# The last projection in rows over four column groups, the mean taken off ahead of it, the last gate kept as rows

## The chip, the cores and the metric

The kernel runs on one core of a Trainium2 chip. The metric is the device time of one execution in microseconds (us). TensorE is called PE here (its weight loads PEld), VectorE DVE, ScalarE ACT, GpSimd POOL and SyncE SP. SP issues all DMA transfers of this kernel. SBUF tiles have 128 partitions; matrix products go to PSUM, which has eight banks of 512 f32 per partition.

## The reference

One decode step of a block with two halves, for a batch of four tokens (B = 4, D = 512). `c` gives six modulation vectors; the first half is attention with 32 heads over a cache of 4096 keys, the second a gated MLP with F = 1792 (half of it, Fh, is 896).

```python
mod = (_silu(c) @ w_mod).reshape(c.shape[0], 6, 1, -1)
sa, ca, ga, sb, cb, gb = (mod[:, 0].copy(), ..., mod[:, 5].copy())
h = _layernorm(x, axis=-1) * (1 + ca) + sa
x = x + ga * _A_ref(h, A_k_cache, A_v_cache, A_wq, A_wo)
h = _layernorm(x, axis=-1) * (1 + cb) + sb
x = x + gb * _B_ref(h, B_w_in, B_w_sp, B_b_sp, B_w_out)

def _B_ref(x, w_in, w_sp, b_sp, w_out):          # one token: S = 1
    z = _gelu(jnp.einsum('bsd,df->bsf', x, w_in))
    z1 = z[..., :Fh].copy()
    z2 = _layernorm(z[..., Fh:], axis=-1)
    g = jnp.einsum('ts,bsf->btf', w_sp, z2) + b_sp[None, :, None]
    return jnp.einsum('bsf,fd->bsd', z1 * g, w_out)
```

With one token per batch entry, w_sp and b_sp are single numbers. So the output is x1 + gb * (w_sp * rstd * ((z1 * (z2 - mean)) @ w_out) + b_sp * (z1 @ w_out)), where x1 is x after the attention and mean and rstd are those of z2.

## The kernel before

**Loads.** The caches hold 268 MB and are read in 16 pairs of tiles, one pair for a group of 8 heads of one batch entry, in three large SBUF buffers (`kv[0]` to `kv[2]`) that take turns. Ahead of them come w_mod and wq, which lie in kv[2] first (L335, L417 to L422); behind them come wo, w_in and w_out, in kv[2] again (L663 to L668): wo in three parts, w_in in four (one for each j, 128 rows of the 512), w_out in three (its row tiles 0 to 3, 4 to 5 and 6). kv[0] is free of cache tiles near the end, and the small tiles of the last stages are cut out of it (L346).

**Start.** The six modulation vectors are made by `mod_part` as products of w_mod (stationary, 128 columns at a time) with silu(c) (`sT`), so they come out with the 512 features over the partitions: `modT[:, oc]` is 128 x (4 feature tiles x 4 batch entries). The last of them, the gate gb, is multiplied by w_sp and b_sp into `gwb` (L545). The queries are made next (L546 to L549).

**Attention.** A loop over the tiles (L636): DVE multiplies keys by the query, PE folds them, softmax, PE multiplies values in four column groups (`values`, L605): each product has only 32 stationary columns, and `tile_position=(0, 32 * t)` puts it in one of four strips of the array, with its output in the 32 PSUM partitions below it.

**End.** `output` multiplies by wo; x1 is made with features over the partitions (L715 to L717), with its layer norm. The products with w_in (L742) run over j, then over the two halves (s = 1 is z2, s = 0 is z1), then over seven row tiles jf: 56 products of 128 stationary columns, with 8 moving columns (batch entries twice, for a part with and without rstd), or 4 for the last j. After j = 1 stands one f32 product (L753) that transposes x1 into rows, 16 x 128, one row for a batch entry and feature tile; DVE copies them to `xr` (L757). GELU on ACT gives z2 (L761) and z1 (L763). DVE spreads z2 over 16 columns (`z2r`, L768), PE sums z2 (L773) and its products with itself (L775), DVE multiplies z1 by z2 into `u[:, :, 0]`, beside z1 in `u[:, :, 1]` (L776), and PE multiplies both with w_out: 28 products with 128 stationary columns of w_out and 8 moving columns (L778). DVE makes mean and rstd (L787 to L801). The result has features over the partitions. One product gives b_sp's part of it, transposed into rows on PE (L812); z1*z2's part less mean times z1's is transposed by another (L823); DVE adds x1 and stores (L822 to L830).

**Order.** Each engine runs its instructions in the order in which the code adds them. `Program.add` (L54) and `depend` (L75) find the waits: `region` (L18) describes each operand by its partitions and the range from its first to its last byte, so a strided view counts with all that lies between its ends, and in PSUM whole banks count for each 32 partitions. PE's instructions signal only where `done` or `sem` says so. `mm` (L384) adds a product with its weight load, `weights` and `moving` the two apart. POOL instructions also wait for the one before last.

Of the kernel before, what the change touches and what calls it, by code (L numbers as in the profile page):

```python
# [7 lines left out]
BF16 = mybir.dt.bfloat16  # L8
# [244 lines left out]
def kernel(  # L253
# [62 lines left out]
    modT = sb.tile([P, 6, J, B], F32, name="modT")  # L316
    qbc = sb.tile([P, NQ, DH], BF16, name="qbc")
    x1b = sb.tile([P, 2, J, B], F32, name="x1b")
# [3 lines left out]
    gwb = sb.tile([P, 3, J, B], F32, name="gwb")  # L322
    sT = sb.tile([P, J, B], BF16, name="sT")


    fill = sb.tile([P, 96], BF16, name="fill")
# [8 lines left out]
    wm, wq, hbc, rows, ones_b, xb, xcT, sg, hn = parts(  # L335
        kv[2], 0, J * 6 * D, J * H * DH, J * B * 64, D, P, *(2 * n * J * B for n in (2, 2, 1, 1)),
    )
    xcT = xcT.bitcast(F32).rearrange("p (j b) -> p j b", j=J)
# [7 lines left out]
    ones_f, ident_f, oP, h, u, zt, z2, z2r, qo, yo, ot, xr, ro, x1p = parts(  # L346
        kv[0], 0, P, 2 * P, 8 * NH // 2 * B, 2 * JB, 2 * JF * B, 4 * JF * B, JF * (B + 4), JF * JB, JB, JB,
        P, 2 * P, 2 * P, 2 * JB,
    )
    ident_f, zt, xr, ro, x1p = (t.bitcast(F32) for t in (ident_f, zt, xr, ro, x1p))  # L350
# [24 lines left out]
    def dve(name, *args, **kw):  # L375
        return prog.call("DVE", name, *args, **kw)
# [82 lines left out]
    for t in (mx, hbc, osb):  # L459
        pool("memset", t, 0.0)  # L460
# [6 lines left out]
        "tensor_reduce", out=maskb[0:J * B], axis=AX.X, op=ADD,  # L467
        in_=ident[0:J * B, 0:J * B].rearrange("p (b j) -> p b j", j=J),
# [233 lines left out]
    pool("memset", z2[:, :, B:B + 1], 1.0)  # L702
# [12 lines left out]
    x1, sq = x1b[:, 0], x1b[:, 1]  # L715
# [14 lines left out]

    rows_ps = {n: bank[0:J * B, 0:P] for n, bank in (("x", po_b), ("c", attn_b), ("a", s_b[2]))}
    rstd = deviation(st, "ln2")
    x1p = x1p.rearrange("p (b j) -> p b j", b=B)
    dve("tensor_copy", out=x1p.rearrange("p b j -> p j b"), in_=x1)
# [51 lines left out]
    zs = sb.tile([P, 8], F32, name="zs")[0:JB]  # L786
    dve(  # L787
        "scalar_tensor_tensor", out=zs[:, 0:B], in0=sq_ps[:, 0:B], scalar=1.0 / FH, in1=maskb[0:JB],
# [4 lines left out]
    total = sb.tile([P, B], F32, name="total")  # L793
    dve("tensor_reduce", out=total, in_=cut(small, JF, B).rearrange("p j b -> p b j"), axis=AX.X, op=ADD)
# [5 lines left out]
    act("activation", out=rstd, in_=zs[:, B + 2:B + 3], func=AF.Ln, bias=eps[0:JB], scale=-1.0)  # L800
    rstd_done = act("activation", out=rstd, in_=rstd, func=AF.Exp, scale=-0.5)  # L801
    dve(
        "scalar_tensor_tensor", out=gwb[:, 1], in0=gwb[:, 0], scalar=-1.0 / FH, in1=bc(total, J),
        op0=MULT, op1=MULT,
    )


    qo, yo = (t.rearrange("p (b j) -> p b j", b=B) for t in (qo, yo))
    dve(
        "tensor_tensor", out=yo.rearrange("p b j -> p j b"), in0=y_ps[:, :, 1], in1=gwb[:, 2], op=MULT,  # L810
    )
    mm(rows_ps["c"], yo.rearrange("p b j -> p (b j)"), ident, True, True, True)  # L812
    dve(
        "tensor_tensor", out=gwb[:, 0:2], in0=y_ps.rearrange("p j e b -> p e j b"), in1=gwb[:, 0:2],
        op=MULT,
    )
    dve(
        "tensor_tensor", out=qo.rearrange("p b j -> p j b"), in0=gwb[:, 0], in1=gwb[:, 1], op=ADD,
    )
    ro, ot = ro[0:JB], ot[0:JB]  # L820

    dve("tensor_tensor", out=ro, in0=rows_ps["c"], in1=xr, op=ADD, after=[rstd_done])  # L822
    mm(rows_ps["a"], qo.rearrange("p b j -> p (b j)"), ident, True, True, True)  # L823
    dve(
        "scalar_tensor_tensor", out=ot, in0=rows_ps["a"], scalar=rstd, in1=ro, op0=MULT, op1=ADD,
    )
    prog.add(
        "SP", lambda e, it: e.dma_start(out=out.rearrange("b s (j p) -> (b s j) p", p=P), in_=ot),
# [49 lines left out]
```

## Time and profile before

| | us |
|---|---|
| median of three runs (662.53 to 662.73) | 662.6 |
| the profiled execution | 662.62 |
| its span in the trace | 660.8 |
| PE / DVE / ACT / POOL busy | 394.6 / 392.7 / 27.3 / 2.6 |
| granted TensorE clock, mean | 0.799 |
| HBM read at 428 GB/s over the span | 282.73 MB |
| last instruction of the program proper (issue of the store) | 658.52 |

Times in the trace count from the start of the span. In the slices of the span, each digit is a busy share, or for PEclk the granted clock, in tenths. A line of the timeline gives start, length, engine, line, operation, output <- inputs and shape; its bracket says how long the engine had been idle and what released it. Nearly all instructions are recorded by helpers, so their line is L160 for DVE and ACT, and L386, L391 and L396 for `mm`, `weights` and `moving`. Tiles cut out of the three large buffers all appear as `kv`, PSUM banks as `bank`. The shape of a product begins with rows * columns of the weights, so `128*32` marks one in a column group. An f32 product appears as two passes.

### The profile page before, as it was taken

The numbers are of one execution on the slowest core, as the hardware profiler recorded it, in microseconds if no ns is written. First come the engines' busy times: TensorE is split into PE (matmuls) and PEld (weight loads), VectorE is DVE, ScalarE is ACT, GpSimd is POOL, SyncE is SP. The second block draws the span as 40 slices with busy tenths as digits, with TensorE's granted clock in tenths as the row PEclk, the third lists the DMA queues.
The fourth block names the chain that finished last, engine by engine and source line by source line (L and its number), as shares of the span: only waits on it lengthen the run. The fifth ranks groups of instructions, "written<-read, shape, count | busy, mean of one in ns | idle before, by whom it ended". The sixth has DMA issues, their size and how long they took to land.

```text
span 660.8 us, 5144 instructions
## 1 busy us (share of the span) xinstructions
PE 394.6 (60%) x2724; PEld 79.7 (12%) x1753; DVE 392.7 (59%) x344; ACT 27.3 (4%) x64; POOL 2.6 (0%) x11
## 2 busy tenths in 40 slices
PE   1628385563848556383855638386563938646875
PEld 1300101010010101001010100101010010101114
DVE  2058292864829386482937648293764829376953
ACT  1100000000000000000000000000000000000002
POOL 1000000000000000000000000000000000000000
PEclk9959787687968768797776879877687987768995
DMA  9999999999999999999999999999999999999996
GB/s 377 446 440 436 414 428 440 436 441 440 428 417 440 436 440 440 428 420 440 436 436 440 436 424 428 440 432 444 432 428 424 440 436 440 436 428 413 438 412 279
DMA packets 7324, 282.86 MB, mean 428 GB/s; under 512 B 780, under 2 KB 916, under 8 KB 2708
## 3 DMA queue, kind: packets, MB, share of 16 engines
q1 hardware_dynamic: 7316, 282.74, 99.1%
q8 instruction: 7, 0.11, 0.1%
q14 instruction: 1, 0.01, 0.0%
HBM read 282.73 MB, written 0.00 MB: 428 GB/s over the span
## 4 chain that ended last, share of the span: by engine, by line
DMA 61%; PE 24%; DVE 12%; another core or an unknown queue 2%; issue 1%; SPq 0%; ACT 0%; DVEq 0%
DMA kv<-in_A_k_cache_dram 57%; PE bank L396 23%; DVE kv L160 12%; DMA kv<-in_A_wo_dram 4%; PE bank L386 1%; SPq L166 0%; DVE S L160 0%; ACT E L160 0%; DVE mx L160 0%; DVE x1b L160 0%; ACT kv L160 0%; DVE rsh L160 0%; DVE mT L160 0%; DVE nm L160 0%
## 5 line engine op out<-in xcount | busy, mean ns | idle before, releaser
L160 DVE TENSOR_TENSOR kv<-kv,qbc 128x8192 bf16<-128x8192 bf16 x64 | 280.2, 4419 | 187.0 <-DMA kv<-in_A_k_cache_dram 187.0
L396 PE MATMUL bank<-kv,ident 128*128 128x512 bf16 x1024 | 259.6, 416 | 162.5 <-DVE kv L160 162.4
L386 PE MATMUL bank<-kv,Ph 128*32 128x512 bf16 x1024 | 89.0, 524 | 0.9 <-DMA kv<-in_A_v_cache_dram 0.9
L160 DVE TENSOR_REDUCE S<-bank 128x64 f32<-128x512 f32 x64 | 43.8, 684 | 36.2 <-PE bank L396 36.2
L386 PE MATMUL bank<-rsh,mean_d 128*128 128x8 f32 x32 | 9.3, 365 | 79.0 <-DVE rsh L160 79.0
L391 PEld LDWEIGHTS <-ident 128*128 128x128 bf16 x65 | 7.7, 118 | 300.9 <-issue 300.9
L160 DVE TENSOR_TENSOR Ph<-E,mask 128x2048 bf16<-128x2048 f32 (+1 forms) x19 | 36.9, 1954 | 10.7 <-ACT E L160 10.7
L386 PEld LDWEIGHTS bank<-kv,Ph 128*32 128x32 bf16 x1024 | 32.9, 127 | 49.6 <-issue 41.0
L160 ACT ACTIVATE E<-S,nm 128x256 f32<-128x256 f32 x16 | 8.1, 507 | 456.7 <-DVE nm L160 456.7
L386 PEld LDWEIGHTS bank<-rsh,mean_d 128*128 128x128 f32 x32 | 7.8, 304 | 141.5 <-DVE rsh L160 141.1
L386 PEld LDWEIGHTS bank<-sel,osb 128*128 128x128 f32 x136 | 17.8, 191 | 55.4 <-issue 54.6
L386 PE MATMUL bank<-sel,osb 128*128 128x8 f32 x136 | 16.3, 246 | 0.4 <-ACT osb L160 0.4
L160 ACT COPY osb<-bank 128x512 f32<-128x512 f32 x16 | 9.4, 586 | 137.5 <-PE bank L386 137.5
L386 PE MATMUL bank<-kv 128*32 128x512 bf16 (+2 forms) x139 | 9.8, 416 | 1.2 <-DMA kv<-in_A_wq_dram 0.8
L396 PE MATMUL bank<-kv,kv 128*128 128x4 bf16 (+1 forms) x212 | 7.0, 168 | 2.4 <-DMA kv<-in_A_wo_dram 2.1
L386 PE MATMUL bank<-ident,kv 8*128 8x8 bf16 (+2 forms) x10 | 0.9, 186 | 11.6 <-DMA kv<-in_A_x_dram 11.3
L391 PEld LDWEIGHTS <-kv 128*128 128x128 bf16 x212 | 6.7, 107 | 3.2 <-DMA kv<-in_A_wo_dram 2.3
L160 DVE TENSOR_REDUCE mx<-S 128x1 f32<-128x256 f32 x16 | 6.7, 420 | 0.5
L160 DVE COPY kv<-bank 128x32 f32<-128x32 f32 (+1 forms) x2 | 0.5, 230 | 9.7 <-ACT kv L160 9.7
L160 DVE RECIPROCAL rz<-bank 128x8 f32<-128x8 f32 x17 | 3.3, 196 | 4.5 <-PE bank L386 4.5
L386 PE MATMUL bank<-sT,kv 128*128 128x4 bf16 x96 | 3.7, 169 | 2.1 <-DVE modT L160 1.8
L386 PEld LDWEIGHTS bank<-kv 128*32 128x32 bf16 (+2 forms) x139 | 4.1, 107 | 6.4 <-issue 2.3
(86 smaller groups left out, 56.2 us busy)
## 6 DMA issues: line engine op xcount, KB each, us to landing
kv<-in_A_k_cache_dram SPq DMA_DIRECT2D x2, 4096.0 KB, 20.2
kv<-in_A_v_cache_dram SPq DMA_DIRECT2D x2, 4096.0 KB, 32.3
kv<-in_A_wq_dram SPq DMA_DIRECT2D x1, 4096.0 KB, 17.9
kv<-in_w_mod_dram SPq DMA_DIRECT2D x1, 3072.0 KB, 10.0
kv<-in_A_wo_dram SPq DMA_DIRECT2D x1, 2560.0 KB, 22.7
kv<-in_B_w_in_dram SPq DMA_DIRECT2D x4, 448.0 KB, 12.9
kv<-in_A_wo_dram SPq DMA_DIRECT2D x1, 1024.0 KB, 24.7
kv<-in_A_wo_dram SPq DMA_DIRECT2D x1, 512.0 KB
```

Source lines behind the costliest of these rows:

```text
L160: return getattr(e, name)(*args, **kw, **(dyn(it) if dyn else {}))
L386: "PE", lambda e, it: e.matmul(out, lhsT=lhsT, rhs=rhs, start=start, stop=stop, **kw),
L391: prog.add("PE", lambda e, it: e.ldweights(lhsT), [lhsT], [], done=False)
L396: return e.add_instruction(mybir.InstMatmult(name=nc.get_next_instruction_name(), engine=mybir.EngineType.PE, ins=[e.lower_ap(rhs), e.lowe ...
```

## The change

The tiles of the last stage get 32 columns for each row tile, of which every eighth holds a batch entry (`cols`) and the others are zero. So a product with 32 stationary columns yields 32 rows, four of them in use, and four such products, one for each quarter t of the 512 output features, fill the four column groups: row 32 t + 8 b holds feature tile t of batch entry b.

- The last gate is made in that form at the start, by 16 products with silu(c) stationary (`sTp`), and copied to `gate` (128 x 128, f32); `modT` holds five vectors and `gwb` is gone.
- x1 goes into rows by four f32 products with `x1p` stationary, at the place of the one before. The copy to `xr` moves behind the products with w_out in the code, and DVE comes to it after the multiply that makes u.
- Sums of z2 are accumulated over jf in four columns (`total`); the sums of squares and of z2 use 28 products in column groups, with no copy of z2.
- DVE takes the mean off z2 (`zc`) before it multiplies by z1.
- Products with w_out have u as the stationary operand and 128 columns of w_out as the moving one, 56 in four column groups: first the part for b_sp (e = 1), then the other (e = 0), for row tiles 0 to 5, then both for row tile 6. They go to two PSUM banks.
- The two banks are multiplied by b_sp or w_sp and the gate, x1 is added, the other part is multiplied by rstd and added, and 16 rows, every eighth, are stored.

```diff
-    modT = sb.tile([P, 6, J, B], F32, name="modT")
+    modT = sb.tile([P, 5, J, B], F32, name="modT")
-    gwb = sb.tile([P, 3, J, B], F32, name="gwb")
-    sT = sb.tile([P, J, B], BF16, name="sT")
+    gate = sb.tile([P, P], F32, name="gate")
...
+    W = 32
+    cols = slice(0, W, W // B)
...
+    sTp = sTp.rearrange("p (j n) -> p j n", j=J)
+    sT = sTp[:, :, cols]
...
-    for t in (mx, hbc, osb):
+    for t in (mx, sTp, hbc, osb):
         pool("memset", t, 0.0)
...
-        "tensor_reduce", out=maskb[0:J * B], axis=AX.X, op=ADD,
-        in_=ident[0:J * B, 0:J * B].rearrange("p (b j) -> p b j", j=J),
+        "tensor_reduce", out=maskb, axis=AX.XY, op=ADD,
+        in_=ident.rearrange("p (t b k) -> p b t k", t=J, b=B),
...
-    for oc in range(2, 6):
+    for oc in range(2, 5):
         mod_part(oc)
+
+    for j in range(J):
+        for t in range(J):
+            c0 = 5 * D + t * P
+            mm(
+                small[W * t:W * t + W, 0:P], sTp[:, j], wm[:, j, c0:c0 + P], j == 0, j == J - 1,
+                j == t == J - 1, tile_position=(0, W * t),
+            )
+    dve("tensor_copy", out=gate, in_=small[:, 0:P])
     mm(cut(small, 2), ones_b, wb_t, True, True, True)
     dve("tensor_copy", out=wbf, in_=cut(small, 2))
-    for k in range(2):
-        dve("tensor_scalar_mul", out=gwb[:, 2 * k], in0=modT[:, 5], scalar1=wbf[:, k:k + 1])
...
-    pool("memset", z2[:, :, B:B + 1], 1.0)
+    u = u.rearrange("p (j e n) -> p j e n", e=2, n=W)
+    x1p = x1p.rearrange("p (j n) -> p j n", j=J)
+    for t in (u, z2, x1p):
+        pool("memset", t, 0.0)
+    pool("memset", z2[:, :, W:W + 1], 1.0)
...
-    dve("tensor_copy", out=x1p.rearrange("p b j -> p j b"), in_=x1)
+    dve("tensor_copy", out=x1p[:, :, cols], in_=x1)
...
             if j == 1 and s == 0:
-                mm(rows_ps["x"], x1p.rearrange("p b j -> p (b j)"), ident_f, True, True, True)
+                for t in range(J):
+                    mm(
+                        po_b[W * t:W * t + W, 0:P], x1p[:, t], ident_f, True, True, t == J - 1,
+                        tile_position=(0, W * t),
+                    )
...
-    xr = xr[0:J * B]
-    dve("tensor_copy", out=xr, in_=rows_ps["x"])
...
-    z2, z2_1 = z2[:, :, 0:B], z2[:, :, 0:B + 1]
-    act("activation", out=z2, in_=zt[:, 1], func=AF.Gelu_apprx_tanh)
-    u = u.rearrange("p (j e b) -> p j e b", e=2, b=B)
-    act("activation", out=u[:, :, 1], in_=zt[:, 0], func=AF.Gelu_apprx_tanh)
+    z1c, z2c = u[:, :, 1, cols], z2[:, :, cols]
+    act("activation", out=z2c, in_=zt[:, 1], func=AF.Gelu_apprx_tanh)
+    act("activation", out=z1c, in_=zt[:, 0], func=AF.Gelu_apprx_tanh)
...
-    z2r = z2r.rearrange("p (j m) -> p j m", j=JF)
+    total = small[:, 0:B]
+    weights(ones_f)
+    for jf in range(JF):
+        moving(total, ones_f, z2c[:, jf], jf == 0, jf == JF - 1, jf == JF - 1)
+    sq_ps = s_b[2][:, 0:B + 1]
+    for jf in range(JF):
+        for t in range(J):
+            mm(
+                sq_ps[W * t:W * t + W], z2[:, jf, 0:W], z2[:, jf, 0:W + 1:W // B], jf == 0, jf == JF - 1,
+                jf == JF - 1 and t == J - 1, tile_position=(0, W * t),
+            )
+    zc = zc.rearrange("p (j b) -> p j b", b=B)
     dve(
-        "tensor_copy", out=z2r.rearrange("p j (b k) -> p j b k", b=B),
-        in_=z2[:, :, :, None].to_broadcast([P, JF, B, J]),
+        "scalar_tensor_tensor", out=zc, in0=bc(total, JF), scalar=-1.0 / FH, in1=z2c, op0=MULT, op1=ADD,
     )
-    sq_ps = s_b[2][0:JB, 0:B + 1]
-    mm(cut(small, JF * B), ones_f, z2, True, True, True)
-    for jf in range(JF):
-        mm(sq_ps, z2r[:, jf], z2_1[:, jf], jf == 0, jf == JF - 1, jf == JF - 1)
-    dve("tensor_tensor", out=u[:, :, 0], in0=u[:, :, 1], in1=z2, op=MULT)
-    y_ps = cut(zo_b, J, 2, B)
-    for j0, j1 in JFS:
-        for jf in range(j0, j1):
-            for jo in range(J):
-                mm2(
-                    y_ps[:, jo], wout[:, jf, jo * P:(jo + 1) * P], u[:, jf],
-                    jf == 0 and jo == 0, jf == JF - 1, jf == JF - 1 and jo == J - 1,
-                )
+    dve("tensor_tensor", out=u[:, :, 0, cols], in0=z1c, in1=zc, op=MULT)
+    y_ps = [zo_b[:, 0:P], attn_b[:, 0:P]]
+    for j0, j1 in ((0, JFS[-1][0]), JFS[-1]):
+        for e in (1, 0):
+            for jf in range(j0, j1):
+                for t in range(J):
+                    mm(
+                        y_ps[e][W * t:W * t + W], u[:, jf, e], wout[:, jf, t * P:(t + 1) * P], jf == 0,
+                        jf == JF - 1, jf == JF - 1 and t == J - 1, tile_position=(0, W * t),
+                    )
+    dve("tensor_copy", out=xr, in_=po_b[:, 0:P])
...
-    total = sb.tile([P, B], F32, name="total")
-    dve("tensor_reduce", out=total, in_=cut(small, JF, B).rearrange("p j b -> p b j"), axis=AX.X, op=ADD)
...
-    dve(
-        "tensor_tensor", out=yo.rearrange("p b j -> p j b"), in0=y_ps[:, :, 1], in1=gwb[:, 2], op=MULT,
-    )
-    mm(rows_ps["c"], yo.rearrange("p b j -> p (b j)"), ident, True, True, True)
...
-    mm(rows_ps["a"], qo.rearrange("p b j -> p (b j)"), ident, True, True, True)
+    for e, t in ((1, t1), (0, t0)):
+        dve(
+            "scalar_tensor_tensor", out=t, in0=y_ps[e], scalar=wbf[:, e:e + 1], in1=gate,
+            op0=MULT, op1=MULT,
+        )
+
+    dve("tensor_tensor", out=t1, in0=t1, in1=xr, op=ADD, after=[rstd_done])
+    dve("scalar_tensor_tensor", out=ot, in0=t0, scalar=rstd, in1=t1, op0=MULT, op1=ADD)
     prog.add(
-        "SP", lambda e, it: e.dma_start(out=out.rearrange("b s (j p) -> (b s j) p", p=P), in_=ot),
+        "SP", lambda e, it: e.dma_start(
+            out=out.rearrange("b s (t n) -> t (b s) n", n=P), in_=ot[::W // B],
+        ),
```

More of the change, by code (lines that the diff above doesn't have):

```diff
@@ L315 @@
     oT = sb.tile([P, 1 + NQ, NH], BF16, name="oT")
-    modT = sb.tile([P, 6, J, B], F32, name="modT")
+    modT = sb.tile([P, 5, J, B], F32, name="modT")
     qbc = sb.tile([P, NQ, DH], BF16, name="qbc")
-    x1b = sb.tile([P, 2, J, B], F32, name="x1b")
     wbm = sb.tile([P, 2 + B], F32, name="wbm")
@@ L321 @@
     xT = sb.tile([P, J, B], F32, name="xT")
-    gwb = sb.tile([P, 3, J, B], F32, name="gwb")
-    sT = sb.tile([P, J, B], BF16, name="sT")
-    fill = sb.tile([P, 96], BF16, name="fill")
+    gate = sb.tile([P, P], F32, name="gate")
+    fill = sb.tile([P, 48], BF16, name="fill")
     kv = [sb.tile([P, NT * DH], BF16, name=f"kv{a}") for a in range(3)]
@@ L332, in parts @@
             a += n
-    wm, wq, hbc, rows, ones_b, xb, xcT, sg, hn = parts(
-        kv[2], 0, J * 6 * D, J * H * DH, J * B * 64, D, P, *(2 * n * J * B for n in (2, 2, 1, 1)),
-    )
+    W = 32
+    cols = slice(0, W, W // B)
+    wm, wq, hbc, rows, ones_b, sTp, xb, xcT, sg, hn = parts(
+        kv[2], 0, J * 6 * D, J * H * DH, J * B * 64, D, P, J * W, *(2 * n * J * B for n in (2, 2, 1, 1)),
+    )
+    sTp = sTp.rearrange("p (j n) -> p j n", j=J)
+    sT = sTp[:, :, cols]
     xcT = xcT.bitcast(F32).rearrange("p (j b) -> p j b", j=J)
@@ L345 @@
     JB = J * B
-    ones_f, ident_f, oP, h, u, zt, z2, z2r, qo, yo, ot, xr, ro, x1p = parts(
-        kv[0], 0, P, 2 * P, 8 * NH // 2 * B, 2 * JB, 2 * JF * B, 4 * JF * B, JF * (B + 4), JF * JB, JB, JB,
-        P, 2 * P, 2 * P, 2 * JB,
+    ones_f, oP, h, u, z2, ot, *parts_f = parts(
+        kv[0], 0, P, 8 * NH // 2 * B, 2 * JB, 2 * JF * W, JF * (W + 2), P,
+        *(2 * n for n in (2 * JF * B, JF * B, 2 * JB, P, J * W, P, P, P)),
     )
-    ident_f, zt, xr, ro, x1p = (t.bitcast(F32) for t in (ident_f, zt, xr, ro, x1p))
+    zt, zc, x1b, ident_f, x1p, xr, t0, t1 = (t.bitcast(F32) for t in parts_f)
     banks = [pm.tile([P, 512], F32, name=f"bank{a}") for a in range(8)]
@@ L710 @@
         output(a, b)
-    x1, sq = x1b[:, 0], x1b[:, 1]
+    x1, sq = (t.rearrange("p (j b) -> p j b", b=B) for t in (x1b[:, 0:JB], x1b[:, JB:2 * JB]))
     dve("tensor_tensor", out=x1, in0=attn_ps, in1=modT[:, 2], op=MULT)
@@ L729 @@
             dve("tensor_tensor", out=xs[:, J - 1], in0=xs[:, J - 1], in1=ms[:, J - 1], op=SUB)
-    rows_ps = {n: bank[0:J * B, 0:P] for n, bank in (("x", po_b), ("c", attn_b), ("a", s_b[2]))}
     rstd = deviation(st, "ln2")
-    x1p = x1p.rearrange("p (b j) -> p b j", b=B)
-    dve("tensor_copy", out=x1p.rearrange("p b j -> p j b"), in_=x1)
+    dve("tensor_copy", out=x1p[:, :, cols], in_=x1)
     dve("tensor_tensor", out=xs[:, J - 1], in0=xs[:, J - 1], in1=rstd, op=MULT)
@@ L776 @@
-    dve("tensor_tensor", out=u[:, :, 0], in0=u[:, :, 1], in1=z2, op=MULT)
-    y_ps = cut(zo_b, J, 2, B)
-    for j0, j1 in JFS:
-        for jf in range(j0, j1):
-            for jo in range(J):
-                mm2(
-                    y_ps[:, jo], wout[:, jf, jo * P:(jo + 1) * P], u[:, jf],
-                    jf == 0 and jo == 0, jf == JF - 1, jf == JF - 1 and jo == J - 1,
-                )
-    zs = sb.tile([P, 8], F32, name="zs")[0:JB]
+    total = small[:, 0:B]
+    weights(ones_f)
+    for jf in range(JF):
+        moving(total, ones_f, z2c[:, jf], jf == 0, jf == JF - 1, jf == JF - 1)
@@ new lines @@
+    y_ps = [zo_b[:, 0:P], attn_b[:, 0:P]]
[8 more added lines that the diff above has]
+    dve("tensor_copy", out=xr, in_=po_b[:, 0:P])
+    zs = sb.tile([P, 8], F32, name="zs")
@@ L787 @@
     dve(
-        "scalar_tensor_tensor", out=zs[:, 0:B], in0=sq_ps[:, 0:B], scalar=1.0 / FH, in1=maskb[0:JB],
+        "scalar_tensor_tensor", out=zs[:, 0:B], in0=sq_ps[:, 0:B], scalar=1.0 / FH, in1=maskb,
         op0=MULT, op1=MULT,
@@ L799 @@
     )
-    act("activation", out=rstd, in_=zs[:, B + 2:B + 3], func=AF.Ln, bias=eps[0:JB], scale=-1.0)
+    act("activation", out=rstd, in_=zs[:, B + 2:B + 3], func=AF.Ln, bias=eps, scale=-1.0)
     rstd_done = act("activation", out=rstd, in_=rstd, func=AF.Exp, scale=-0.5)
-    dve(
-        "scalar_tensor_tensor", out=gwb[:, 1], in0=gwb[:, 0], scalar=-1.0 / FH, in1=bc(total, J),
-        op0=MULT, op1=MULT,
-    )
-    qo, yo = (t.rearrange("p (b j) -> p b j", b=B) for t in (qo, yo))
-    dve(
-        "tensor_tensor", out=yo.rearrange("p b j -> p j b"), in0=y_ps[:, :, 1], in1=gwb[:, 2], op=MULT,
-    )
-    mm(rows_ps["c"], yo.rearrange("p b j -> p (b j)"), ident, True, True, True)
[L813 to L822, printed above, removed]
-    mm(rows_ps["a"], qo.rearrange("p b j -> p (b j)"), ident, True, True, True)
-    dve(
-        "scalar_tensor_tensor", out=ot, in0=rows_ps["a"], scalar=rstd, in1=ro, op0=MULT, op1=ADD,
-    )
+    for e, t in ((1, t1), (0, t0)):
[5 more added lines that the diff above has]
+    dve("scalar_tensor_tensor", out=ot, in0=t0, scalar=rstd, in1=t1, op0=MULT, op1=ADD)
     prog.add(
-        "SP", lambda e, it: e.dma_start(out=out.rearrange("b s (j p) -> (b s j) p", p=P), in_=ot),
+        "SP", lambda e, it: e.dma_start(
+            out=out.rearrange("b s (t n) -> t (b s) n", n=P), in_=ot[::W // B],
+        ),
         [ot], [], sem="any_out", dma=True,
```

## The prediction

> **What bounds the kernel now.** I read the page first: its slices and its chain of waits.
>
> ```profile
> PEclk9959787687968768797776879877687987768995
> ...
> DMA 61%; PE 24%; DVE 12%; another core or an unknown queue 2%; issue 1%; SPq 0%; ACT 0%; DVEq 0%
> ```
>
> Loads fill the time until the last slice, and none of them is edited, so the change can only act in what follows the last loads. That is the chain after 650 us (start, length, what):
>
> ```profile
> 653.65 0.54 PE bank L386 x2
> 654.19 0.32 PE bank L396 x7
> ...
> 655.96 0.33 PE bank L386 x7
> 656.28 0.88 PE bank L396 x28
> ...
> 657.43 0.29 PE bank L386
> ...
> 658.16 0.34 DVE kv L160
> ```
>
> It names in order the x transpose, products with w_in, z2 statistics, products with w_out, a transpose at the end, and the sum that is stored. Next come the loads beside it: issues on SP, then the times from issue to landing.
>
> ```profile
> 641.71 0.43 SPq L166 DMA_DIRECT2D kv<-in_B_w_in_dram  x1
> ...
> 643.89 1.20 SPq L166 DMA_DIRECT2D kv<-in_B_w_out_dram  x1
> ```
> ```profile
> kv<-in_B_w_in_dram SPq DMA_DIRECT2D x4, 448.0 KB, 12.9
> ...
> kv<-in_B_w_out_dram SPq DMA_DIRECT2D x1, 128.0 KB, 12.9
> ```
>
> The last part of w_in lands at 641.71+12.9 = 654.6 and the last of w_out at 643.89+12.9 = 656.8. In narrow windows PE loads its first weights of w_in's last part at 654.70, though the part before was issued out at 654.57: 0.13 us of slack. The last four products with w_out wait for 656.8 too, and lose almost nothing. The timeline gives the durations:
>
> ```profile
> 653.58 0.61 PE L386 MATMUL bank<-kv 128*16 128x128 f32 x2
> ...
> 655.65 0.63 PE L386 MATMUL bank<-kv 128*128 128x28 bf16 x8 [0.32 <-ACT kv L160]
> ...
> 656.22 0.93 PE L396 MATMUL bank<-kv,kv 128*128 128x8 bf16 x28
> ...
> 658.52 0.35 SPq L828 DMA_DIRECT2D out_dram<-kv  x1
> ```
>
> Last, windows (engines' busy time and counts, then granted clock), one of the attention's value products in four column groups, one of the end:
>
> ```profile
> 108.00:110.00 2.00, 2.00 (x24) 0.77 (x20) 0.00 (x0) 0.00 (x0) 0.00 (x0) 0.50 1.21 524
> ...
> 656.00:657.00 1.00, 1.00 (x35) 0.97 (x35) 0.68 (x7) 1.00 (x1) 0.00 (x0) 0.50 0.12 42
> ```
>
> Both are at clock 0.50. In the first, 20 weight loads (five groups of four) go out in 2 us: single starts are 0.427 us apart from group to group, 3 to 7 ns apart within one. So four column groups stream 512 columns at once in 0.427 us; 128 columns take 0.107 at this clock, and 0.054 at full clock, where the same groups are 0.215 apart.
>
> **The change part by part.** Times are against this profiled execution: span 660.8 in 662.62, so 1.8 around it; the three runs' median is 662.6, the same.
>
> Front. Removed: 16 products for the last gate (0.58), its copy 0.17, two multiplies 0.37. Added: 16 products of 128 columns in four groups (at 0.107 a group 0.43, plus 0.27 to finish), one 128x128 copy (0.27 by the x-row copy), a memset on POOL (by 0.95 for 128x1024, 0.12) and 128 instead of 16 partitions in one reduce (0.26 by the mask's). The last query must wait for wq anyway: PE sits idle from 19.86 to 20.62. By rows the new chain ends near 20.2. Cost 0. Were that cover gone, some 0.3 us would move the queries' end at 29.3, which has until 41.1, when the first k tile is there.
>
> Middle. Three memsets on POOL (448, 238 and 256 bf16 columns; by the 0.95 row about 0.9 us) follow 637.9; the first reader is the x copy at 652.95. Cost 0; no SP issue waits for them.
>
> The x rows, now four f32 products of 32 columns, two passes each, in column groups, ahead of w_in's third part. Now: first pass 653.58, second 0.19 later, next weights 654.12, 0.54 in all. A pass takes 0.19 by these starts; by what f32 products gain from 16 to 32 columns (0.393 to 0.423), 0.24; I take 0.21, with 0.14 to leave. In the order issued, a group's second pass must wait for its first, while the next group's first pass can run beside it: five steps, 5x0.21+0.14 = 1.19, so 0.65 more, less 0.13 slack: **+0.52**. No f32 row in column groups exists. Lower end: all passes hidden in one group's time, 0. Upper end: eight in a row, 8x0.21+0.14 = 1.82, +1.15. I take the middle because the bf16 groups start within 7 ns of each other. A gain is excluded: w_in's last part lands when it lands. The Trainium skill ("TensorEngine Tiling (Array Packing)", Tiling Modes) says that tiles operate independently, so different tiles load and multiply in parallel; by that the sum is as taken, without it the upper end holds. The bf16 rows agree, and no run here shows it for f32.
>
> GELU to the first w_out product. z2's GELU ends at 655.60; the copy (0.27) that the statistics waited for goes. Seven products of the column sums start at 655.65 at 0.027 each, and the last is finished at 655.98. Then DVE takes the mean off (start 656.02, 0.185 as the 128x28 rows) and multiplies by z1 (656.23 to 656.41); PE sees it at 656.46 (DVE to PE, 0.05). Both orders of products wait for it: their weights are slices of u, and a strided write counts over its whole range, so also the columns that need only z1 stand behind the multiply. Before, the first weights were loaded at 656.21: **+0.25**. The 28 statistics products lie in this gap: by the 16 in column groups at 644.64 (0.31 with a 0.18 finish) 0.25, one after another at 0.025 each 0.70, ending at 656.1 or 656.54; so 0 to +0.08, I take 0.
>
> Products with w_out: 28 at 0.027, 0.76 from first to last start with the landing, become 14 groups of four at 0.107, 13x0.107+0.01 = 1.40: **+0.64**. The landing at 656.8 is past by then: the last two groups start near 658.3. Weight loads of 32 columns are hidden, as in the rows with 512; were they not, 0.15 by the longest load of that form, so up to +0.56 more. The last product finishes 0.28 after its start (the 128-column transpose: 0.27), before 0.17: **+0.11**.
>
> Last result to the store's issue, 657.15 to 658.52, was 1.38. It loses two transposes and three small multiplies and becomes four 128x128 instructions on DVE. Call the last result T. The first multiply needs the other bank, ready at T-0.11: it starts at T-0.07 and takes 0.34 (the row of the final sum, also with a per-partition scalar); the second overlaps by 0.07 and ends at T+0.54; the add 0.28, starting 0.02 later for the wait on rstd; the final one 0.035 later, 0.34, ends at T+1.22; issue T+1.24: **-0.14**. With 0.28 in place of 0.34 it would be -0.3. The x copy and the sums for rstd fit in before T: rstd is done near 657.8 plus the x delay, 0.9 ahead of the add. The store has 16 rows of 256 bytes as before: 0, or 0.1 either way by the spread of issues (0.25 to 0.47).
>
> Sum: 0.52+0.25+0.64+0.11-0.14 = **+1.38**, 664.0.
>
> **The rivals.**
> Serial f32: the x passes of different groups do not overlap. +1.15 in place of +0.52: 664.6. For it: no f32 row in groups, and the two passes now stand one after the other. Against: bf16.
> Hidden x: the passes all overlap, 0 in place of 0.52: 663.5. Against: the 0.19 between passes in one group.
> The other side: the clock returns to 1.00 for the end. In the trace it changes only at points 3.41 us apart; the last change is at 644.83, the next points are 651.66 and 655.07. From 651.66 on, x would cost 0.64 and stay within the slack, groups 0.054: last result at 656.46+0.70+0.22 = 657.38, store at 658.62, 662.7, not slower. From 655.07 only: +0.6, 663.2. It decides only if the step comes by 655.07. Against: PE is busy for 1.00 of 1.00 us in the window at 656 and the clock is still 0.50, and all PE work up to 655 but x is what it was. The Trainium skill ("TensorE: Matmul & The Clock Gate", Part 1) says that some 3.4 us of sustained activity bring the full rate; by that rule the denser end would run fast. The windows from 646 to 657 at 0.50 with PE mostly busy do not bear it out for such small products.
> Faster by over 0.2% needs 1.3 us out of the 1.7 between the last landing and the store, against four DVE instructions of 1.2 us: nothing in the trace does that.
>
> **How the numbers follow.** 0.2% is 1.3 us here, about what a measurement of this kernel can tell from no change; the line is at 663.93. The forecast has 0.54 (663.6 to 664.3; 0.35 of it over the line, since what is left out are waits, 0.19 under), serial f32 0.30, hidden x 0.10, the clock 0.05, faster 0.01. Slower 0.35+0.30 = 0.65, same 0.19+0.10+0.05 = 0.34, faster 0.01. The range runs from 663.2 (late clock step, or hidden x with short multiplies) to 664.8 (serial f32 with 0.2 of uncovered waits).
>
> **What would show it.** The profile after should show: the x rows as eight f32 passes 128*32 over about 1.1 us and w_in's last part starting near 655.2; the first multiply of u before the first w_out product; 56 products 128*32 over 1.4 us at clock 0.50; no transposes after 657; the store's issue near 659.9; no difference before 650. Wrong would make it: a granted clock of 1.00 after 655, x passes in a row, or groups of w_out products far from 0.107.

## The result and the profile after

The changed kernel takes 664.34 us (median of 12 runs, 663.83 to 664.67), the kernel before 662.72 us (median of 12, 662.43 to 663.88): a ratio of 1.0021 with a 95% interval of 1.0012 to 1.003, slower by about 0.2%. The median lies 0.4 us above the prediction's line at 663.93, but the interval has values on both sides of 1.002, so it does not show that the change costs more than 0.2%. The time lies inside the predicted range and 0.3 us above the predicted 664.0. The profiled execution of the changed kernel took 664.26 us with a span of 662.4, against 662.62 and 660.8 before.

From the page of the changed kernel, the granted clock and the DMA engines' busy share by slices, and the shares of the chain that ended last:

```profile
PEclk9959777686977768697786869778686977868995
DMA  9999999999999999999999999999999999999996
...
DMA 61%; PE 22%; DVE 14%; another core or an unknown queue 2%; issue 1%; SPq 0%; ACT 0%
```

Loads still fill the time up to the last slices. The chain of waits behind them (start, length, what) now reads:

```profile
653.75 0.59 PE bank L389 x8
654.33 0.32 PE bank L399 x7
...
654.68 0.20 DVE kv L160
...
654.92 0.36 PE bank L399 x7
...
655.53 0.34 ACT kv L160
...
655.91 0.34 PE bank L399 x7
...
656.27 0.21 DVE kv L160
...
656.50 0.29 DVE kv L160
...
656.84 1.61 PE bank L389 x27
...
658.47 0.14 DVE kv L160
...
658.74 0.55 DVE kv L160 x2
...
659.31 0.35 DVE kv L160
```

It names the x rows, seven products with w_in's third part, a DVE step, the last part of w_in, GELU, the sums of z2, the two DVE steps that make u, the products with w_out, and four DVE instructions. The two transposes of the chain before are gone. Between the third and the last part of w_in the chain of the kernel before has a DVE step too:

```profile
654.19 0.32 PE bank L396 x7
...
654.53 0.20 DVE kv L160
...
654.77 0.36 PE bank L396 x7
```

The timeline of the changed kernel has the shapes:

```profile
653.68 0.66 PE L389 MATMUL bank<-kv 128*32 128x128 f32 x8
...
655.53 0.55 ACT L160 ACTIVATE kv<-kv 128x28 bf16<-128x28 f32 x2 [0.53 <-DVE kv L160]
...
656.27 0.20 DVE L160 SCALAR_TENSOR_TENSOR kv<-bank,kv 128x28 f32<-128x28 f32 x1 [0.55 <-PE bank L399]
656.50 0.28 DVE L160 TENSOR_TENSOR kv<-kv 128x28 bf16<-128x28 bf16 x1
...
656.84 1.68 PE L389 MATMUL bank<-kv,kv 128*32 128x128 bf16 x56 [0.31 <-DVE kv L160]
...
658.47 0.61 DVE L160 SCALAR_TENSOR_TENSOR kv<-bank,wbm,gate 128x128 f32<-128x128 f32 x2 [1.05 <-PE bank L389]
659.00 0.28 DVE L160 TENSOR_TENSOR kv<-kv 128x128 f32<-128x128 f32 x1
659.31 0.35 DVE L160 SCALAR_TENSOR_TENSOR kv<-kv,zs 128x128 bf16<-128x128 f32 x1
659.69 0.67 SPq L831 DMA_DIRECT2D out_dram<-kv  x1
```

The eight f32 passes are nearly as short as two were, 0.66 against 0.61. Two GELUs take 0.55 together, 0.44 before. SP works for 0.67 on the store, 0.35 before. One more view, a window of the changed kernel (busy time and count of PE, PEld, DVE, ACT and POOL, then granted clock, DMA share, GB/s), shows the clock in the midst of the new products:

```profile
656.90:657.90 1.00, 1.00 (x44) 1.00 (x48) 0.48 (x5) 0.89 (x3) 0.00 (x0) 0.50 0.00 0
```

Single instructions of both traces give the difference step by step (us). "Seen" is when ACT, which waits for the store at the end of the program, goes on.

| step | before | after | difference | predicted |
|---|---|---|---|---|
| first x pass starts at | 653.577 | 653.677 | +0.10 | 0 |
| from there to the first product of w_in's last part | 1.195 | 1.244 | +0.05 | +0.52 |
| to the start of z2's GELU | 0.603 | 0.606 | 0 | 0 |
| to the first product with w_out | 0.840 | 1.311 | +0.47 | +0.25 |
| first to last start of these products | 0.765 | 1.368 | +0.60 | +0.64 |
| the last one's finish | 0.168 | 0.314 | +0.15 | +0.11 |
| to the store's issue | 1.377 | 1.174 | -0.20 | -0.14 |
| issue to seen | 1.375 | 1.762 | +0.39 | 0 |
| to the end of the span | 0.940 | 0.941 | 0 | 0 |
| sum | | | +1.56 | +1.38 |

Three terms differ: the x rows cost nearly nothing, and two costs that the prediction did not have, 0.2 ahead of w_out and 0.4 at the store, stand in their place.

### The profile page after: what moved, and what is told of

Read it like the earlier page. It is cut to its first block, busy times and chain, and to the rows that moved or that the text cites. A ratio compares the mean times of both kernels' runs of the same rounds, so it can differ in the third digit from the quotient of the medians.

```text
span 662.4 us, 5257 instructions
## 1 busy us (share of the span) xinstructions
PE 396.1 (60%) x2783; PEld 80.6 (12%) x1806; DVE 392.6 (59%) x339; ACT 27.4 (4%) x64; POOL 3.8 (1%) x15
## 4 chain that ended last, share of the span: by engine, by line
DMA 61%; PE 22%; DVE 14%; another core or an unknown queue 2%; issue 1%; SPq 0%; ACT 0%
DMA kv<-in_A_k_cache_dram 57%; PE bank L399 21%; DVE kv L160 14%; DMA kv<-in_A_wo_dram 4%; PE bank L389 1%; SPq L166 0%; DVE S L160 0%; ACT E L160 0%; DVE mx L160 0%; ACT kv L160 0%; DVE rsh L160 0%; DVE nm L160 0%; DVE mT L160 0%; DVE hm L160 0%
## 5 line engine op out<-in xcount | busy, mean ns | idle before, releaser
L389 PE MATMUL bank<-kv 128*32 128x512 bf16 (+4 forms) x261 | 13.9, 325 | 2.7 <-DVE modT L160 1.8
L389 PEld LDWEIGHTS bank<-kv 128*32 128x32 bf16 (+2 forms) x261 | 7.4, 112 | 9.2 <-issue 3.5
L160 POOL MEMSET kv<- 128x128 bf16 (+5 forms) x7 | 2.5, 352 | 634.7 <-PE bank L389 634.3
## 6 DMA issues: line engine op xcount, KB each, us to landing
kv<-in_B_w_in_dram SPq DMA_DIRECT2D x4, 448.0 KB, 12.8
```

The source lines that it names most:

```text
L160: return getattr(e, name)(*args, **kw, **(dyn(it) if dyn else {}))
L389: "PE", lambda e, it: e.matmul(out, lhsT=lhsT, rhs=rhs, start=start, stop=stop, **kw),
```

## The experiments

Theory after the two traces: products in column groups do not wait for one another in the order issued, so the f32 passes overlap; what is new in the GELUs and in the multiply is that they write 2-byte values that lie apart; the store pays for its pattern. The rivals are named with each run. All edits but one are against the changed kernel, and "after" below is its trace. The loads shift by several tenths from trace to trace (the first x pass starts between 653.58 and 654.60), so terms of 0.1 to 0.4 are read from steps inside the traces; the medians are given beside them. The 95% interval of every ratio below overlaps that of the change (1.0012 to 1.003), so the medians alone do not settle any of these causes: what the experiments show, they show by steps of one trace each.

**The x rows all in one column group.**

```diff
-    po_b[W * t:W * t + W, 0:P], x1p[:, t], ident_f, True, True, t == J - 1,
-    tile_position=(0, W * t),
+    po_b[0:W, t * P:(t + 1) * P], x1p[:, t], ident_f, True, True, t == J - 1,
+    tile_position=(0, 0),
```

> The changed kernel with the four f32 products of x all in the first column group, side by side in one bank (the copy then takes wrong rows). Theory: in the changed kernel the second passes ran beside one another, so x cost two pass times, 0.24 from the first to the last start; in one group they are in a row, eight passes of 0.21: 1.5 from first to last start, x to the first product of w_in's last part 2.4 to 2.5 instead of 1.24, and the span grows by 1.2, the price that the prediction gave to the serial rival. Rival: passes of f32 products overlap in one group too, or x is hidden by the landing: no change.

Measured: 665.36 us, ratio to before 1.0032 (1.0021 to 1.0044). The timeline of this kernel:

```profile
653.58 1.92 PE L389 MATMUL bank<-kv 128*32 128x128 f32 x8
```

From first to last of the eight starts it is 1.495 us, in after 0.235; from the first pass to w_in's last part 2.501, in after 1.244. So column groups are worth 1.26 us here, all that a row of eight costs, and none of it is covered: both differences are 1.26. In after the four first passes start within 0.020 us, the four second ones within 0.020, from 0.215 on: a group's second pass does hold up its own group, but not the first passes of the groups behind it. That the two passes of a product are issued one behind the other is an assumption, as a pass's record does not tell its group; the next run does not need it.

**Order of the groups.** The group t becomes the outer loop, so the products of one group are issued behind one another.

```diff
-            for jf in range(j0, j1):
-                for t in range(J):
+            for t in range(J):
+                for jf in range(j0, j1):
```

> The changed kernel with the w_out products of one column group issued one after another (t outside, jf inside). Theory from the trace of the changed kernel, where the first passes of four f32 products start together: the groups do not wait for the order of issue among themselves, each runs its own products. Then the 56 still take about 1.4 us from first to last start, up to 2 if only few can be held. Rival, as predicted: starts follow the order of issue, so that only neighbours at the end of a run of six overlap: 8 runs of 0.53, about 4.5 us, and the span grows by 3.

Measured: 665.11 us, ratio 1.0035 (1.0023 to 1.0048). The timeline:

```profile
656.89 2.39 PE L389 MATMUL bank<-kv,kv 128*32 128x128 bf16 x56 [0.31 <-DVE kv L160]
```

First to last start 2.077 us, against 1.368 in after and 4.5 if a product had to wait for all issued ahead of it. Within the first 0.51 us twelve products start, where the six of the first group, 0.107 apart, would have been alone. With 0.107 us for a product in its group, 55 x 0.107 / 2.077 gives 2.8 products under way at a time: later groups start ahead of waiting products of earlier ones, but only so far.

**Half the columns.** Each product with w_out streams 64 columns instead of 128.

```diff
-    y_ps = [zo_b[:, 0:P], attn_b[:, 0:P]]
+    y_ps = [s_b[3][:, 0:P], attn_b[:, 0:P]]
...
-    y_ps[e][W * t:W * t + W], u[:, jf, e], wout[:, jf, t * P:(t + 1) * P], jf == 0,
+    y_ps[e][W * t:W * t + W, 0:P // 2], u[:, jf, e], wout[:, jf, t * P:t * P + P // 2], jf == 0,
```

> The changed kernel with 64 instead of 128 moving columns in each w_out product, the right half of each quarter of the output left out (and y_ps[0] in another bank). Theory: at clock 0.50 a group of four is bound by its 128 columns, 0.107 us. Then groups come 0.053 apart, the 56 products take 0.70 from first to last start instead of 1.37, and the span falls by 0.7. Rival: they are bound by the weight loads or by issue. Then 1.37 stays.

Measured: 663.78 us, ratio 1.0012 (1.0003 to 1.0022). The timeline:

```profile
656.79 1.05 PE L389 MATMUL bank<-kv,kv 128*32 128x64 bf16 x56 [0.31 <-DVE kv L160]
```

First to last start 0.803 us, where 0.70 was expected. Groups start 0.053 apart, half of 0.107, but for one gap: the 42nd product starts 0.12 late, which is the whole excess (this gap comes up again in the last section). So the columns set the pace at 128 and at 64, and the weight loads are hidden at both.

**Data columns side by side.** The four columns in use of each row tile lie side by side, in place of every eighth; the indices of the statistics follow (not shown). The stored rows are those of after.

```diff
-    cols = slice(0, W, W // B)
+    cols = slice(0, B)
...
-    z1c, z2c = u[:, :, 1, cols], z2[:, :, cols]
+    z1c, z2c = u[:, :, 1, cols], z2[:, :, 2:2 + B]
```

> The changed kernel with the four batch entries in adjacent columns (0 to 3 of each 32) instead of every eighth; the store still takes every eighth row, most of which hold no results. Theory: ACT and DVE write single bf16 values at a distance slower than neighbours. Then the GELUs fall from 0.33 to 0.23 each, the multiply into u from 0.28 to 0.18, and the first w_out product comes 1.11 us after the first GELU's start instead of 1.31; the span falls by 0.2. Rival: the 0.1 has to do with the larger tiles or their place. Then all of them stay.

Measured: 664.71 us, ratio 1.0026 (1.0016 to 1.0036). The timeline:

```profile
656.23 0.44 ACT L160 ACTIVATE kv<-kv 128x28 bf16<-128x28 f32 x2 [1.18 <-DVE kv L160]
...
657.09 0.19 DVE L160 TENSOR_TENSOR kv<-kv 128x28 bf16<-128x28 bf16 x1
```

The GELUs take 0.228 and 0.226 (after: 0.327, 0.322; before: 0.226 both), the multiply 0.188 (0.278; 0.174), and the first product comes 1.094 us after GELU's start instead of 1.311: the 0.22 that the prediction lacked. The time does not show it. In this trace the loads are later, which hides it: the first x pass starts 0.31 later than in after, and w_in's last part follows 1.617 behind it instead of 1.244. Whether the other executions had late loads too, no trace shows.

**u in two halves.** The columns that need only z1 lie in one range, those that need z2 in another, so that products for b_sp need not wait for the multiply.

```diff
-    u = u.rearrange("p (j e n) -> p j e n", e=2, n=W)
+    u = u.rearrange("p (e j n) -> p j e n", e=2, n=W)
```

> The changed kernel with u laid out as all of z1*z2 and then all of z1, so that the two no longer lie inside one another's range. Theory: the w_out products with z1 stood behind DVE's multiply only for that. Then the first w_out product comes right behind the statistics, 0.87 us after the first GELU's start instead of 1.31, the 56 products still take 1.37 from first to last start, and the span falls by 0.44. Rival: PE was held by the landing of w_out or by the statistics. Then 1.31 stays.

Measured: 664.24 us, ratio 1.0021 (1.0011 to 1.0031). GELU's start to the first product falls from 1.311 to 0.840, the whole 0.47 expected, so the wait was the overlap of the written range. The products take 1.506 instead of 1.368, since the 42nd starts 0.18 late. From the first x pass to the end of the span it is 8.38 against 8.72, so 0.34 of the expected 0.44 is left in the trace; the median is 0.10 below that of the change, and the ratio is the same.

**The other part's work ahead.** u in halves as above; all products of the b_sp part first, their gate and x1 worked in while the others run, and rstd folded into the per-partition scalar: two DVE instructions behind the last product.

```diff
-    for j0, j1 in ((0, JFS[-1][0]), JFS[-1]):
+    for j0, j1 in ((0, JF),):
...
-    dve("tensor_tensor", out=t1, in0=t1, in1=xr, op=ADD, after=[rstd_done])
-    dve("scalar_tensor_tensor", out=ot, in0=t0, scalar=rstd, in1=t1, op0=MULT, op1=ADD)
+    dve("scalar_tensor_tensor", out=t1, in0=y_ps[1], scalar=wbf[:, 1:2], in1=gate, op0=MULT, op1=MULT)
+    dve("tensor_tensor", out=t1, in0=t1, in1=xr, op=ADD)
+    wr = zs[:, B + 2:B + 3]
+    dve("tensor_tensor", out=wr, in0=rstd, in1=wbf[:, 0:1], op=MULT, after=[rstd_done])
+    dve("scalar_tensor_tensor", out=t0, in0=y_ps[0], scalar=wr, in1=gate, op0=MULT, op1=MULT)
+    dve("tensor_tensor", out=ot, in0=t0, in1=t1, op=ADD)
```

> The changed kernel with u laid out as all of z1*z2 and then all of z1, all products with z1 ahead of all with z1*z2, b_sp's part and x1 added while the latter run, and rstd times w_sp taken into the last multiply, so that two instead of four large DVE instructions follow the last product. Theory: the first w_out product 0.84 us after the first GELU's start, 1.37 to 1.5 from first to last start, last result to store 0.72 instead of 1.17: the span 0.8 to 0.9 below the changed kernel's, still some 0.7 above that of before. Rival: the gains do not add up because the wait moves to w_out's last landing or to rstd: under 0.5.

Measured: 664.15 us, ratio 1.0013 (1.0004 to 1.0023). GELU's start to the issue is 3.404 us, 4.167 in after and 3.150 before. The chain's tail:

```profile
659.12 0.29 DVE kv L160
...
659.41 0.10 DVE zs L160
...
659.55 0.36 DVE kv L160
...
659.94 0.29 DVE kv L160
```

Last result to issue is 0.831, not 0.72: the small multiply (`zs`) still stands in the way. The 25th product, the first to need w_out's last part, starts 0.10 late, because that part lands only then (at 658.34). So the steps gain 0.76, but the median is only 0.2 below that of the change, where 0.8 to 0.9 was expected. In the profiled execution (664.74) late loads hide the gain: the first x pass starts 0.92 later than in after, and w_in's last part follows 1.628 behind it. No trace tells it for the other executions.

**Both cuts.** The kernel above, with the data columns adjacent.

```diff
-    cols = slice(0, W, W // B)
+    cols = slice(0, B)
```

> The two cuts together: the part for b_sp issued first with x1, rstd folded in and u split in halves, as in the kernel that had an issue 3.40 us after GELU's start, and the four data columns of a row tile adjacent, which took 0.10 from a GELU (the rows stored are every eighth as before, which then are not the ones that hold the result). If the steps add up, z2's GELU takes 0.226 and the first product with w_out comes 0.74 after its start, where it was 0.84 (the 35 statistics products stand between the two and start 0.10 earlier); products 1.42, last result to issue 0.83, so the issue comes 3.30 after GELU's start, where the kernel before has 3.15 (0.84 + 0.77 + 0.17 + 1.38). With the store still 0.39 longer and x as in the changed kernel the sum from the first x pass to the end is 7.85 against 7.26 before: still 0.5 to 0.6 slower than the kernel before if the loads land alike, 0.1% or less in the median. Rival: the first product waits for z1's GELU and not for the statistics, so that 0.62 is reached and the issue comes 3.2 after GELU's start.

Measured: 663.96 us, ratio 1.001 (0.9998 to 1.0022). GELU's start to the first product 0.760, then 1.452, 0.314 and 0.823: the issue comes 3.349 us after GELU's start, near the 3.30 of the theory; the rival's 0.62 is not reached. From the first x pass to the end it is 7.90 against 7.26 before. Of the 1.16 by which its span (662.00) is over that of before, 0.64 is this and 0.53 a later first x pass. So even with these cuts the form is not ahead of the kernel before by its trace, and by the ratio the two can't be told apart. What is left is mostly the products (+0.69, of which 0.13 is again the wait for w_out's last part) and the store (+0.39).

**The store's destination.** One plain run of rows, as before; the source still every eighth partition.

```diff
-            out=out.rearrange("b s (t n) -> t (b s) n", n=P), in_=ot[::W // B],
+            out=out.rearrange("b s (j p) -> (b s j) p", p=P), in_=ot[::W // B],
```

> The changed kernel, with the same 16 rows stored to consecutive places of the output (so the output is permuted). In the changed kernel the store's issue took 0.67 us on SP and the end was seen 1.76 us after its start; before, 0.35 and 1.38. Theory: the cost is the two strides of the destination. Then 0.35 and 1.38 come back, and the span falls by 0.39. Rival: it is the source, every eighth partition. Then 0.67 and 1.76 stay.

**The store's source.** The first 16 partitions; the destination as in after.

```diff
-            out=out.rearrange("b s (t n) -> t (b s) n", n=P), in_=ot[::W // B],
+            out=out.rearrange("b s (t n) -> t (b s) n", n=P), in_=ot[0:4 * B],
```

> The changed kernel with the store taking rows 0 to 15 instead of every eighth row (the output is then wrong), the destination as in the changed kernel. With the destination of before the store's issue was still 0.57 and the end seen 1.74 after it. Theory now: the source, partitions eight apart, costs it; then 0.35 and 1.38 come back, and the span falls by 0.39. Rival: neither pattern, but the time or state in which SP finds itself at the end; then 0.6 and 1.75 stay.

**Both sides plain.**

```diff
-            out=out.rearrange("b s (t n) -> t (b s) n", n=P), in_=ot[::W // B],
+            out=out.rearrange("b s (j p) -> (b s j) p", p=P), in_=ot[0:4 * B],
```

> The changed kernel with only the store edited on both of its sides: the source is the first 16 rows of the tile in place of every eighth, and the destination is one plain run of 16 rows of 128 values, as in the kernel before (the values stored are then not those of the reference). Source alone (0.74 us on SP, 1.84 from the issue until ACT sees the end) and destination alone (0.57, 1.74) left the store about as long as the change has it (0.67, 1.76). Theory: either side that departs from one plain run of rows is enough to cost the 0.3 on SP; with both plain it is as before the change: about 0.35 on SP and 1.38 until seen, so the end comes 0.39 earlier after the issue. Rival: it is not the pattern but what SP or its queue stands in at that moment; then 0.6 to 0.7 and about 1.75 stay. Products, GELUs and DVE's tail as in the changed kernel either way (GELU to first product 1.31, products 1.37, last result to issue 1.17).

**The kernel before, with the new order of the rows in its store.**

```diff
-        "SP", lambda e, it: e.dma_start(out=out.rearrange("b s (j p) -> (b s j) p", p=P), in_=ot),
+        "SP", lambda e, it: e.dma_start(out=out.rearrange("b s (j p) -> j (b s) p", p=P), in_=ot),
```

> The kernel before, with only the store's destination changed: its 16 rows go out in the order of the feature tiles (four steps of 512 bytes, four steps of rows), as the changed kernel does, where they were one plain run (so the values end up in other places than the reference has them). Theory (the pattern costs it): SP takes 0.6 to 0.7 for the issue in place of 0.35, ACT sees the end 1.75 after it in place of 1.38, and the span is 0.35 to 0.4 longer than before if the loads land alike. Rival (the moment, not the pattern): 0.35 and 1.38 as before. Everything ahead of the store as in the kernel before.

Measured, with the engines counted by the burst of semaphore writes with which the store's transfers end (where it is 4, one more write comes 0.6 us ahead of them):

| store | SP busy | issue to seen | engines | time, us | ratio to before (95%) |
|---|---|---|---|---|---|
| before: both plain | 0.347 | 1.375 | 16 | 662.72 | |
| after: both in steps | 0.667 | 1.762 | 4 | 664.34 | 1.0021 (1.0012 to 1.003) |
| destination plain | 0.574 | 1.743 | 16 | 664.76 | 1.0027 (1.0016 to 1.0038) |
| source plain | 0.742 | 1.841 | 4 | 664.72 | 1.0022 (1.0012 to 1.0031) |
| both plain | 0.347 | 1.364 | 16 | 664.0 | 1.0016 (1.0006 to 1.0025) |
| before, destination in steps | 0.750 | 1.858 | 4 | 663.33 | 1.0007 (0.9998 to 1.0017) |

The store in the timelines of the last two kernels, first the changed kernel with both sides plain:

```profile
660.06 0.35 SPq L831 DMA_DIRECT2D out_dram<-kv  x1
```

and the kernel before with the new order:

```profile
658.55 0.75 SPq L828 DMA_DIRECT2D out_dram<-kv  x1
```

The first two runs each overturned what they were made for: neither side alone is the cause. (In the trace with the destination plain, 664.85 us, the 42nd product with w_out also starts 0.38 late, so its time tells little of the store.) The last two settle it. Either side in steps is enough, both plain is the old store, and put into the kernel before it costs 0.48 from issue to seen; its span is 661.35, 0.51 over that of before (the ratio's interval has 1 in it, so this rests on the trace). So it is the pattern, and not the state of SP at the end.

The number of engines does not decide it, since with a plain destination there are 16 and it takes 1.743. The Trainium skill ("DMA: Bandwidth & Descriptors", Why a DMA increments its semaphore by 16 and not by 1) says that a transfer uses the largest number of engines up to 16 that divides the outermost sizes of both sides. The records agree: 16 where both are 16, 4 where the destination is 4 by 4. It gives no price for the issue, which is what moved here.

## Why the prediction was right in its total, and where it was not

The time came out as forecast, with the median on the side of the likelier sign and close to its line. That the sum is off by only 0.18 is luck: three terms were off by more and cancelled: x -0.47, GELU to products +0.22, the store +0.39. The others are small (late loads +0.10, products -0.04, finish +0.04, tail -0.06); together +0.18, which is 1.56 less 1.38.

- **Front and middle, cost 0:** right. The last DVE step there ended at 20.34; PE waited until 20.71 for wq. No difference before 650 but 0.10 in the loads.
- **The x rows, +0.52:** the term that failed most; measured +0.05. The failed step is "in the order issued, a group's second pass must wait for its first", taken to hold up also what is issued behind it. The passes of the four groups overlap, so the rival "hidden x" was right about this term, and its lower end, 0, was nearly the price. The argument against that rival, the 0.19 between passes, concerned one group alone. The 0.13 of slack that the prediction took off was not there either: it is what the weight loads waited for the landing, but the products behind them wait for the DVE step in the chain. w_in's last part had landed at 654.65 before and at 654.74 in after, its first product started at 654.77 and 654.92. So the 0.05 that the x rows cost comes through whole. The rule cited of the Trainium skill ("TensorEngine Tiling (Array Packing)", Tiling Modes), that tiles operate independently, is borne out for f32 by the kernel with one group (1.495 against 0.235). The serial rival fell by the same run, in which that step takes 1.26 more.
- **GELU to the first product, +0.25:** the mechanism was right: the products for b_sp stood behind the multiply because of the range of u, and splitting u took away 0.47. The size was off by 0.22, because the GELU, the multiply and the subtraction were priced by rows whose elements lie in runs of four or more. Measured: GELU +0.10, multiply +0.10, subtraction +0.02. The adjacent columns gave 0.217 back.
- **Products with w_out, +0.64 and +0.11:** right, +0.60 and +0.15. Groups start 0.107 apart, read from the attention's products of 512 columns and scaled; weight loads are hidden. The half-width run shows that columns set it.
- **Last result to issue, -0.14:** -0.20; the four took 0.35, 0.34, 0.28 and 0.35, as summed, but the add (659.00) began 0.08 before the second multiply had ended (658.74 + 0.34), an overlap that was counted between the two multiplies only.
- **Store, 0 or 0.1 either way:** failed. "16 rows of 256 bytes as before" looked at the bytes; the issue depends on how the rows lie on both sides. Measured +0.39, outside the bounds given.
- **The clock:** stayed at 0.50 with PE busy for 1.00 of 1.00 us, so that rival did not come. The Trainium skill ("TensorE: Matmul & The Clock Gate", Part 1) has the full rate after some 3.4 us of sustained activity; this trace does not test that, since PE is busy for at most 2.9 us of each 3.4 from 645.9 on.

The range came from adding up ends. The time lies just above the stretch from 663.6 to 664.3 that the forecast's own mechanism was given, in the part kept for serial f32, and not for that reason: an error in one term hid an error in two others. Were x priced right and the rest not, the forecast would have been 663.5 and low.

## What to carry to other kernels

Column groups are the cheap part of such a layout: four small products, f32 too, cost about what one does, as long as neighbours in the order of issue belong to different groups. What the layout drags along has to be priced at every writer and reader: single 2-byte elements written apart, a range that makes early columns wait for late ones, and a store whose rows are no longer one plain run. At the end of a program, where nothing hides it, look at the pattern of the last DMA and not at its bytes.

## What the runs showed of the hardware that was not expected

- TensorE starts products of another column group ahead of a waiting one that was issued earlier: 2.077 us for the 56 products with one group's products behind one another, where strict order gives 4.5. The Trainium skill ("TensorE: Matmul & The Clock Gate", Part 3) has matrix products start and end strictly in program order; these starts differ from that, and the measurement decides here.
- A GELU that writes 28 single bf16 elements per partition, 16 bytes apart, takes 0.327 us in place of 0.226 in runs of four, and a DVE multiply that reads and writes such places 0.278 in place of 0.188, some 3 to 4 ns more for an element. An f32 copy of 16 elements into such places took 0.18, as before.
- SP's issue of a 4 KB store took 0.35 us with one plain run of rows on both sides and 0.57 to 0.75 with any other, and the end was seen 0.37 to 0.48 later.
- In three traces (u in halves, half the columns, destination plain) the 42nd product with w_out started 0.18, 0.12 and 0.38 us late, 1.47, 1.31 and 1.46 us after the end of a 16 KB load that the profile counts in its instruction queue. That load ended 0.26, 0.67 and 0.03 us ahead of the first of these products, in after 1.05 us ahead, with no gap. That PE waited for it was only argued from this order and from the place, the same in the program each time, and not tried.
- w_in's last part came 1.62 us after the first x pass in three traces (adjacent columns, work ahead, store plain on both sides), 1.39 in one and 1.24 in the others but the one with one column group. Where it was 1.62, PE waited for the landing, which came 13.6 to 13.7 us after the issue, where it was 12.8 to 13.0 in the traces with 1.24. The third of the three differs from after in its last instruction alone, so the edits don't make it; why the load took longer stays open.
